# The max pass of an attention kernel in six groups of block pairs instead of eleven pairs, with a new order of all tasks

## The chip, the cores and the metric

The kernel runs on one core of one Trainium2 chip. The metric is the device time of one execution in microseconds, as the median of several runs. One execution was also recorded by the hardware profiler; all rows below are from that one.

## The reference, cut to what matters

```python
def _attn_ref(q, k, v, g_q, g_k):            # q, k, v: 8 x 12 x 448 x 64, fp32
    q_n, k_n = rmsnorm(q, g_q), rmsnorm(k, g_k)
    scores = 1/sqrt(64) * q_n @ k_n.T
    scores = scores - np.max(scores, axis=-1, keepdims=True)
    attn = np.exp(scores)
    attn = attn / (np.sum(attn, axis=-1, keepdims=True) + 1e-09)
    return attn @ v

def reference(...):
    x = attn_out.transpose(0, 2, 1, 3).reshape(3584, 768)
    # group router (4 groups), then expert router (4 experts a group), argmax each;
    # each token: combined * (relu(x @ w1[g, e]) @ w2[g, e]), w1 768x1024, w2 1024x768
```

## The kernel before, in words

The work has two stages that overlap a little: attention, and then a mixture of experts (MoE) on its output, sixteen experts of which each token takes one.

Attention is cut into 16 units, numbered u = 0 to 15; a unit is six heads of one batch. The rows of a unit's queries lie in 21 blocks of 128: for each of three pairs of heads seven blocks, of which the fourth (`TB`, block numbers 3, 10 and 17) is a tail block that holds 64 rows of either head. For a unit the kernel does this: it loads and normalizes k and q and transposes them (the tiles kt, kb, qa, qb); it makes a **max pass** (`plan_max`), in which TensorE multiplies each block of q by the 448 keys of its head (tile pmx, line 522, or line 517 for a tail block) and VectorE takes the maximum of each row (line 527, one reduction for a pair of blocks); the maxima are transposed (pmt) and join the operands of the **scores pass** (pss, lines 585 and 580), so that the exponential on ScalarE (line 595) already has its maximum subtracted; GpSimd or VectorE splits off the low part of the exponentials (pl, line 601); then TensorE multiplies by v (po, line 646), VectorE or ScalarE scales the result (lines 670, 671 or 666), and the output goes to HBM in two halves (xhl, lines 709 and 713). The router and the MoE stage (lines 1417 and 1444 are its two products) read it from there.

The products of the max pass of units 1 to 15 contract over 64 rows only. The two blocks of a pair use the lower and the upper 64 rows of the array (kt and kb hold the same keys in the two halves), so they run side by side. A tail block is two products of 64 columns, one for each head. All other products of the stage use all 128 rows.

PSUM has three buffers of two banks for all of this (`psd=3` in `ROOM`): pmx, pss, the transposes and the router's products take them in turn, so a task that takes one gets the buffer that the third taker before it used, and can start when that one's reader is through.

The order is written out by hand or by a planner outside the kernel: each step is a task with an engine, and `PLAN` gives each task a date (hundredths, in the order in which the tasks are added). `emit` sorts the tasks by their dates, so the dates set the order of the instructions on each engine and nothing else; a "*" picks the second engine for a task that may run on two (GpSimd or VectorE for the low parts, ScalarE or VectorE for the scaling). Each engine then works through its list strictly in that order, waiting on semaphores. The last MoE jobs, from the eleventh, are dated by a formula relative to the planned ones (`Moe.plan`).

In the list of before, a max task is one pair: 11 a unit, (0,1), (2,3), ... (18,19), (20), each of which takes one buffer.

Of the kernel before, what the change touches and what calls it, by code (L numbers as in the profile page):

```python
# [18 lines left out]
ALU = mybir.AluOpType  # L19
AX = mybir.AxisListType  # L20

P = 128
# [90 lines left out]
class Attention:  # L113
# [382 lines left out]

    def pairs_of(self, n, u):
        step = NBK if u == 0 else n
        return [(j, min(j + 2, o + step)) for o in range(0, n, step) for j in range(o, o + step, 2)]

    def plan_max(self, flow, u, B, D):
        nc = self.nc
# [3 lines left out]
        def mm(a, e):  # L506
            f = lambda t: t.rearrange("p n c -> p (n c)")
            s = d["mm", a] = self.ps_d.tile([P, 2, 512], F32, tag="psd", name=f"pmx{u}_{a}")
            for n in range(a, e):
                o = 64 * ((n - a) % 2)  # L510
# [3 lines left out]
                if c == TB:  # L514
                    for r in range(2):
                        x, z = self.blocks(i, r)
                        nc.tensor.matmul(s[r * 64:r * 64 + 64, n - a, 0:448],
                                         qa[:, n * P + r * 64:n * P + r * 64 + 64], kt[:, x:z],
                                         start=True, stop=True)
                else:  # L520
                    x, z = self.blocks(i, int(c > TB))
                    nc.tensor.matmul(s[:, n - a, 0:448], qa[:, n * P:(n + 1) * P], kt[:, x:z], start=True, stop=True)  # L522

        def rd(a, e):
            if "mx" not in d:
                d["mx"] = self.wl.tile([P, N], F32, tag="mx", name=f"mx{u}", bufs=self.ROOM["mx"])
            nc.vector.tensor_reduce(d["mx"][:, a:e], d.pop(("mm", a))[:, 0:e - a, 0:448], axis=AX.X, op=ALU.max)  # L527
# [16 lines left out]
        for a, e in self.pairs_of(N, u):  # L544
            b = Buffer("psd")
            x = flow.add("PE", lambda a=a, e=e: mm(a, e),
                         [*self.of(D, "kmv", a, e), *(self.of(D, "kcp", a, e) if u else []), *self.of(D, "qa", a, e), *firsts],
                         takes=[b] + ([] if a else [B["mx"]]), uses=[B["kt"], B["qa"]] + ([B["kb"]] if u else []))
            firsts = firsts or [x]
            reds.append(flow.add("DVE", lambda a=a, e=e: rd(a, e), [x, *reds[:1]],  # L550
                                 uses=[b, B["mx"]]))
        D["m"] = {}
        for a, e in ((0, 7), (7, 14), (14, 21)) if u == 0 else ((0, N),):
            bx, bm = Buffer("psd"), Buffer("mxt")
            need = [reds[j] for j, (x, z) in enumerate(self.pairs_of(N, u)) if x < e and z > a]
# [692 lines left out]
class Moe:  # L1248
# [222 lines left out]
    def plan_early(self, flow, attn, router, opens):  # L1471
# [13 lines left out]
        g = 0  # L1485
# [59 lines left out]
        self.g, self.last_tr = g, trs[-1]  # L1545
        self.at_read = {(j, i): mm[j, FC - 1] if i < 4 else m2s[j][-1] for j in range(self.JF) for i in range(len(PC))}

    def plan(self, agenda):
# [42 lines left out]
        for j, (k, later, c) in enumerate(J):  # L1591
# [66 lines left out]
441 1 3010 1825 439 4515 9008 12509 4716 963 3009 440 0 474 535 521 600 778 962 1026 1132 1607 1839* 1903 2503 1608  # L1658
1737 2349 1827 3012 475 568 1027 1079 1133 1185 1252 1436 1606 1671 1945 2010* 2454 2685 1736 2174 3366 2336 4127 898
1186 1422 1488 1469 1553 1738 1838 1902 2011 2013 2443* 2686 2874 2337 2395 2875 2502 6207 2012 2586 4938 4436 5381  # L1660
# [196 lines left out]
```

## Time and profile before

| what | value |
|---|---|
| median of 3 runs | 1008.05 us (1004.07 to 1014.55) |
| the profiled execution | 1012.01 us, its span 1010.4 us |
| PE (TensorE's products) busy in the span | 922.1 us, 91% |
| DVE (VectorE) busy | 745.2 us, 74% |
| ACT (ScalarE) busy | 623.8 us, 62% |
| POOL (GpSimd) busy | 566.0 us, 56% |
| last reduction of the max pass starts at | 450.9 us |

The busy times are shares of the whole span; the two stages have different limits, so the views by stretch are to be read beside them. PEld are weight loads; a product's row lasts from its first column in to its last column out, and rows overlap, so the distance from the start of one product to the start of the next tells what it costs the engine.

### The profile page before, as it was taken

To read this page: it belongs to the slowest core of one execution; us is meant where nothing else is said; L and a number is where in the kernel's file an instruction comes from. 1 tells how busy PE (TensorE), PEld (TensorE's weight loads), DVE (VectorE), ACT (ScalarE), POOL (GpSimd) and SP (SyncE) were. 2 spreads that over 40 slices of the span, in tenths; PEclk is the share of its full clock that TensorE was granted. 3 is DMA by queue.
4 is the path that set the end of the run, shared out by engine and by line. 5 is a ranking of instruction groups with operands and counts; after the bars stand their busy time and mean duration, and the time that the engine had idled before them with its cause. 6 is when DMAs were issued, how large, how long until landed. Compare 5 with 4: busy or idle time off the path is not lost.

```text
span 1010.4 us, 28824 instructions
## 1 busy us (share of the span) xinstructions
PE 922.1 (91%) x11761; PEld 656.8 (65%) x11761; DVE 745.2 (74%) x1002; ACT 623.8 (62%) x986; POOL 566.0 (56%) x481
## 2 busy tenths in 40 slices
PE   1699999999998989997896999999989999999995
PEld 1356666666665656655766776777757687778883
DVE  3999999899999899898775275566556785756620
ACT  3788998879987867657553264555446556445520
POOL 4589999989997878885445342223113232435411
PEclk9899999999998999899899999999989999999998
DMA  5776787787897467646897999997979999998910
GB/s 141 185 196 133 194 197 182 164 201 167 218 174 175 114 141 154 106 97 189 208 230 200 275 295 273 325 302 234 289 244 342 302 304 307 301 255 275 285 64 28
DMA packets 223095, 213.78 MB, mean 212 GB/s; under 512 B 129455, under 2 KB 179621, under 8 KB 222960
## 3 DMA queue, kind: packets, MB, share of 16 engines
q1 hardware_dynamic: 213008, 188.23, 70.7%
q0 software_dynamic: 8608, 22.99, 7.1%
q8 instruction: 93, 1.52, 0.7%
q10 hardware_dynamic: 1344, 0.69, 0.3%
q14 instruction: 42, 0.34, 0.1%
HBM read 145.69 MB, written 23.41 MB: 167 GB/s over the span
## 4 chain that ended last, share of the span: by engine, by line
PE 60%; DVE 19%; issue 7%; DMA 5%; ACT 4%; POOL 3%; SPq 2%; POOLq 0%; DVEq 0%; ACTq 0%
PE ps L1444 21%; PE ps L1417 20%; PE po L646 6%; DVE mx L527 5%; PE pss L585 5%; PE pmx L522 3%; DVE vl L374 3%; DVE ss L267 2%; DVE pl L601 2%; DMA nq<-q 1%; DMA stage<-w 1%; DMA tb<-tab 1%; PE pss L580 1%; ACT p L595 1%; PE pkt L303 1%
## 5 line engine op out<-in xcount | busy, mean ns | idle before, releaser
L601 POOL TENSOR_TENSOR pl<-p 128x896 f16<-128x896 f32 (+1 forms) x157 | 262.2, 1691 | 41.2 <-ACT p L595 38.1
L1417 PE MATMUL ps<-mx,w1h 128*128 128x256 f16 (+6 forms) x1728 | 245.1, 258 | 10.3 <-DMA mx<-xg 6.2
L1417 PE MATMUL ps<-mx,w1l 128*128 128x256 f16 (+6 forms) x864 | 212.2, 257 | 0.0
L527 DVE TENSOR_REDUCE mx<-pmx 128x2 f32<-128x896 f32 (+1 forms) x177 | 177.7, 1032 | 10.3 <-PE pmx L522 6.5
L595 ACT ACTIVATE p<-pss 128x896 f32<-128x896 f32 (+1 forms) x177 | 151.6, 884 | 52.8 <-PE pss L585 40.6
L646 PEld LDWEIGHTS <-p 128*128 128x128 bf16 (+1 forms) x3072 | 143.9, 103 | 51.2 <-issue 38.7
L1417 PEld LDWEIGHTS <-w1h 128*128 128x128 f16 x1728 | 155.9, 99 | 29.1 <-issue 14.1
L1444 PE MATMUL ps<-w2h,hh 128*128 128x384 f16 (+2 forms) x768 | 165.0, 306 | 6.9 <-ACT y L1456 6.9
L646 PE MATMUL po<-vh,pl 128*128 128x65 f16 (+1 forms) x1536 | 158.5, 196 | 11.5 <-DVE pl L601 6.1
L1444 PE MATMUL ps<-w2l,hh 128*128 128x384 f16 (+2 forms) x768 | 164.4, 304 | 0.0
L1444 PE MATMUL ps<-w2h,hl 128*128 128x384 f16 (+2 forms) x768 | 164.4, 304 | 0.0
L646 PE MATMUL po<-vh,p 128*128 128x65 f16 (+1 forms) x1536 | 160.9, 200 | 0.8 <-ACT xm L666 0.4
L646 PE MATMUL po<-vl,p 128*128 128x64 f16 (+1 forms) x1536 | 158.8, 196 | 0.0
L1371 DVE SCALAR_TENSOR_TENSOR w1l<-stage,w1h 128x1536 f16<-128x1536 f32 x64 | 113.5, 1797 | 47.9 <-ACT w1h L1369 46.6
L1371 DVE SCALAR_TENSOR_TENSOR w2l<-stage,w2h 128x1536 f16<-128x1536 f32 x64 | 111.5, 1754 | 50.5 <-ACT w2h L1369 50.4
L1444 PEld LDWEIGHTS <-hh 128*128 128x128 f16 (+2 forms) x1536 | 102.0, 101 | 65.1 <-issue 14.1
L1463 POOL DMA_INDIRECT out<-y,tb x23 | 36.7, 1594 | 185.5 <-ACT y L1456 117.0
L646 PEld LDWEIGHTS <-pl 128*128 128x128 f16 (+1 forms) x1536 | 129.2, 103 | 13.1 <-DVE pl L601 7.1
L1424 ACT ACTIVATE hh<-ps 128x256 f16<-128x256 f32 (+6 forms) x144 | 47.6, 348 | 128.4 <-PE ps L1417 119.1
L1369 ACT ACTIVATE w1h<-stage 128x1536 f16<-128x1536 f32 x64 | 93.6, 1480 | 34.9 <-DMA stage<-w 34.9
L585 PE MATMUL pss<-qa,kt 128*128 128x448 f16 x288 | 103.2, 358 | 3.3 <-DVE mx L527 2.1
L1406 POOL DMA_INDIRECT xg<-x,tb x41 | 60.8, 1482 | 80.7 <-DMA mx<-xg 33.8
(209 smaller groups left out, 1628.2 us busy)
## 6 DMA issues: line engine op xcount, KB each, us to landing
stage<-w SPq DMA_DIRECT2D x64, 768.0 KB, 10.2
stage<-w SPq DMA_DIRECT2D x64, 512.0 KB, 6.2
stage<-w SPq DMA_DIRECT2D x64, 256.0 KB, 5.1
vn<-v SPq DMA_DIRECT2D x16, 576.0 KB, 5.1
x<-xhl SPq DMA_DIRECT2D x16, 576.0 KB, 4.5
nk<-k SPq DMA_DIRECT2D x30, 288.0 KB
nq<-q SPq DMA_DIRECT2D x30, 288.0 KB, 3.8
qa<-qh SPq DMA_DIRECT2D x30, 176.0 KB, 3.2
```

The costliest lines, as they stand in the source:

```text
L527: nc.vector.tensor_reduce(d["mx"][:, a:e], d.pop(("mm", a))[:, 0:e - a, 0:448], axis=AX.X, op=ALU.max)
L585: nc.tensor.matmul(s[:, n - a, 0:448], w[:, n * P:(n + 1) * P], mv[:, x:z], start=first, stop=not first)
L595: nc.scalar.activation(p[:, 0:e - a], s, AF.Exp, scale=1.0 / 64)
L601: ENG[eng].tensor_tensor(l[:, 0:n], p[:, 0:n], h[:, 0:n], op=ALU.subtract)
L646: nc.tensor.matmul(o[op, c, 0:nn], w, mv, start=st, stop=sp, skip_group_check=True)
L1369: self.nc.scalar.activation(hi, t, AF.Copy, scale=64.0)
L1371: self.nc.vector.scalar_tensor_tensor(lo, t, 64.0, hi, op0=ALU.mult, op1=ALU.subtract)
L1406: self.nc.gpsimd.indirect_dma_start(g[0:m], None, self.x16[0:n], bass.IndirectOffsetOnAxis(ap=tb[0:m, i, 0:1], axis=0), bounds_check=n - 1 ...
L1417: nc.tensor.matmul(s[:, 0:c], wb[w][:, i, fs], x[:, l + i, o:o + c], start=i + j == 0, stop=i == DC - 1 and j == 2)
L1424: self.nc.scalar.activation(hh, s[:, 0:c], AF.Relu)
L1444: nc.tensor.matmul(s[q * m:q * m + m, 0:n], self.h[h][:, f, a:a + m], wb[w][:, f, o:o + n], start=f + j == 0, stop=f == self.FC - 1 and j ...
L1463: i = self.nc.gpsimd.indirect_dma_start(out, bass.IndirectOffsetOnAxis(ap=idx, axis=0), d.pop(("y", i))[:, 0:self.D // r], None, bounds_ch ...
```

## The change

For units 1 to 15 the max pass is made in six tasks instead of eleven. A task is a group of up to two pairs whose products stand one behind the other on TensorE, and it takes two PSUM buffers at once. Two of the tail blocks, 3 and 10, form a pair of their own, the third, 17, stands alone, and the other blocks are paired without them. There are still eleven reductions a unit, ten for pairs and one for a single block; that of (3,10) writes two columns that aren't neighbours. Each reduction is a task of its own, as before. Unit 0 keeps its pairs.

```diff
+    BATCHES = ((0, 1), (2, 4)), ((5, 6), (7, 8)), ((9, 11), (12, 13)), ((14, 15), (16, 18)), ((19, 20), (3, 10)), ((17,),)
...
-            for n in range(a, e):
-                o = 64 * ((n - a) % 2)
+            for m, n in enumerate(e):
+                o = 64 * m
...
+        def batch(b):
+            for ns in self.BATCHES[b]:
+                mm(ns[0], ns)
+
+        def rd(a, ns):
...
+            step = max(1, ns[-1] - a)
+            nc.vector.tensor_reduce(d["mx"][:, a:ns[-1] + 1:step], d.pop(("mm", a))[:, 0:len(ns), 0:448], axis=AX.X, op=ALU.max)
...
+            for j, ps in enumerate(self.BATCHES):
+                bs = [Buffer("psd") for _ in ps]
+                x = flow.add("PE", lambda j=j: batch(j),
+                             [y for nm in ("kmv", "kcp", "qa") for y in self.of(D, nm, 0, N)] + firsts,
+                             takes=bs + ([] if j else [B["mx"]]), uses=[B["kt"], B["qa"], B["kb"]])
+                firsts = firsts or [x]
+                for b, ns in zip(bs, ps):
+                    reds.append(flow.add("DVE", lambda ns=ns, o=0, w=len(ns): rd(ns[0], ns), [x, *reds[:1]],
+                                         uses=[b, B["mx"]]))
...
-        self.g, self.last_tr = g, trs[-1]
+        self.g, self.last_trs = g, trs
...
-                tg = max(tg, dated(self.last_tr) + 10.0)
+                tg = max(tg, max(map(dated, self.last_trs)) + 10.0)
```

`PLAN` is replaced as a whole: every task of both stages has a new date. The list has 75 tasks fewer, all of them max tasks on TensorE (15 units, 5 each). Read against the tasks, the two lists say the following. In the old one 165 max tasks of units 1 to 15 stand in 152 places on TensorE's list, that is with other products between them; in the new one 90 tasks stand in 88 places. Some steps change engine:

| step | old list | new list |
|---|---|---|
| low part of the exponentials (line 601), 177 tasks | 20 on VectorE | 16 on VectorE, the rest on GpSimd |
| low half of the output (line 713), 16 tasks of two instructions | 5 on VectorE | 2 on VectorE |
| scaling of the result, 48 tasks (one of lines 670 and 671 each on VectorE, seven of line 666 on ScalarE) | 19 on VectorE | 24 on VectorE |
| low part of k (line 298), units 1 to 15, 30 tasks | 3 on VectorE | 4 on VectorE |
| copy of the transposed k (lines 309, 311), 30 tasks | 1 on VectorE | 0 on VectorE |

## Rows read from the trace of the kernel before

**Rows 1.** Busy time by stretch: us from the start, busy (x instructions), clock, DMA.
```profile
75.00:450.00 375.00, 357.88 (x5814) 232.99 (x5812) 356.84 (x488) 304.79 (x538) 330.50 (x224) 0.98 0.73 162
450.00:553.00 103.00, 82.60 (x1097) 64.25 (x1096) 75.77 (x131) 53.76 (x99) 55.33 (x67) 0.94 0.78 196
553.00:1010.00 457.00, 438.85 (x4512) 335.04 (x4510) 255.22 (x302) 215.60 (x278) 135.97 (x117) 0.98 0.85 262
```

**Rows 2.** The chain that ended last, by line, from 75 to 450 us.
```profile
by line: PE po L646 14.6%; DVE mx L527 12.2%; PE pss L585 11.4%; DVE vl L374 7.5%; PE pmx L522 6.5%; issue 5.6%; DVE ss L267 3.9%; DVE pl L601 3.0%; PE pss L580 2.9%; DVE ql L336 2.7%; ACT p L595 2.5%; DVE qp L283 2.3%; PE pqt L324 2.3%; PE
```

**Rows 3.** The same chain from 450 to 553 us.
```profile
by line: issue 37.0%; DMA tb<-tab 12.2%; POOL pl L601 9.0%; POOL tab L1049 6.9%; DVE pl L601 6.3%; DMA mx<-xg 4.4%; DMA xg<-x,tb 2.9%; PE pss L585 2.7%; PE po L646 2.6%; POOL xg L1406 2.5%; DVE ogt L1154 2.3%; DVE vl L374 1.7%; DVE xg L1287
```

**Rows 4.** The same chain from 553 us to the end.
```profile
by line: PE ps L1444 46.9%; PE ps L1417 43.2%; DMA stage<-w 2.9%; issue 1.3%; DVE w1l L1371 1.2%; ACT w2h L1369 0.5%; DVE hl L1426 0.4%; DVE w2l L1371 0.4%; ACT y L1456 0.2%; SPq L1352 0.2%; POOL out L1463 0.2%; ACT hh L1424 0.1%; SPq L1353
```

**Rows 5.** Timeline of PE (start us, us) around a pair that stands alone.
```profile
228.70 0.19 PE L646 MATMUL po<-vl,p 128*128 128x64 f16 x1
228.73 0.20 PE L646 MATMUL po<-vh,pl 128*128 128x65 f16 x1
228.86 0.36 PE L522 MATMUL pmx<-kt,qa 64*128 64x448 f16 x1
228.86 0.36 PE L522 MATMUL pmx<-kb,qa 64*128 64x448 f16 x1
229.15 0.20 PE L646 MATMUL po<-vh,p 128*128 128x65 f16 x1
```

**Rows 6.** Timeline of PE from a pair of which one block is a tail.
```profile
313.96 0.36 PE L522 MATMUL pmx<-kt,qa 64*128 64x448 f16 x1
314.25 0.38 PE L517 MATMUL pmx<-kb,qa 64*64 64x448 f16 x2
314.56 0.36 PE L585 MATMUL pss<-qa,kt 128*128 128x448 f16 x1
314.76 0.35 PE L585 MATMUL pss<-qb,kb 128*128 128x448 f16 x1
```

**Rows 7.** Timeline of PE around two pairs, one behind the other.
```profile
196.81 0.19 PE L646 MATMUL po<-vh,pl 128*128 128x65 f16 x1
196.94 0.36 PE L522 MATMUL pmx<-kt,qa 64*128 64x448 f16 x1
...
197.13 0.35 PE L522 MATMUL pmx<-kt,qa 64*128 64x448 f16 x1
...
197.42 0.20 PE L646 MATMUL po<-vh,p 128*128 128x65 f16 x1
```

**Rows 8.** The tile pmx: its reductions, ns min/median/max, first and last start.
```profile
L527 DVE TENSOR_REDUCE mx<-pmx x177: 608/1082/1094, 32.9 to 450.9; 128x2 f32<-128x896 f32 x159, 128x1 f32<-128x448 f32 x18
```

**Rows 9.** Groups by line: busy us, mean ns of one, idle before.
```profile
L601 POOL TENSOR_TENSOR pl<-p 128x896 f16<-128x896 f32 (+1 forms) x157 | 262.2, 1691 | 41.2 <-ACT p L595 38.1 <-ACT rl L987 2.2 <-PE po L646 0.4
...
L666 ACT ACTIVATE xm<-po,rr 128x64 f32<-128x64 f32 x203 | 44.8, 335 | 13.1 <-DVE rt L1038 5.5 <-DVE po L280 4.2 <-DVE rr L652 3.2
...
L601 DVE TENSOR_TENSOR pl<-p 128x896 f16<-128x896 f32 (+1 forms) x20 | 33.0, 1657 | 2.5 <-ACT p L595 2.5
L713 POOL TENSOR_TENSOR xhl<-xm,xhl 128x1152 f16<-128x1152 f32 (+1 forms) x22 | 33.0, 1520 | 1.5 <-ACT xhl L709 1.4
...
L713 DVE TENSOR_TENSOR xhl<-xm,xhl 128x1152 f16<-128x1152 f32 (+1 forms) x10 | 12.3, 1269 | 2.8 <-ACT xhl L709 2.8
L670 DVE TENSOR_TENSOR xm<-po,rr 128x384 f32<-128x384 f32 x19 | 10.4, 550 | 0.2
...
L671 DVE TENSOR_TENSOR xm<-po,rr 128x64 f32<-128x64 f32 x19 | 4.0, 213 | 0.0
L298 DVE TENSOR_TENSOR kn<-nk,kn 128x448 f16<-128x448 f32 x3 | 3.1, 1021 | 0.0
```

**Rows 10.** What PE waited for from 75 to 450 us: us in total, times, longest.
```profile
PE pmx L522 <- DVE mx L527: 5.9, 5, 4.1
...
PE pmx L522 <- DVE ql L336: 1.9, 3, 1.4
PE pss L585 <- DVE mx L527: 1.9, 4, 1.0
```

More of the change, by code (lines that the diff above doesn't have):

```diff
@@ L521, in mm @@
                     x, z = self.blocks(i, int(c > TB))
-                    nc.tensor.matmul(s[:, n - a, 0:448], qa[:, n * P:(n + 1) * P], kt[:, x:z], start=True, stop=True)
-        def rd(a, e):
+                    nc.tensor.matmul(s[:, m, 0:448], qa[:, n * P:(n + 1) * P], kt[:, x:z], start=True, stop=True)
+        def batch(b):
+            for ns in self.BATCHES[b]:
+                mm(ns[0], ns)
+        def rd(a, ns):
             if "mx" not in d:
                 d["mx"] = self.wl.tile([P, N], F32, tag="mx", name=f"mx{u}", bufs=self.ROOM["mx"])
-            nc.vector.tensor_reduce(d["mx"][:, a:e], d.pop(("mm", a))[:, 0:e - a, 0:448], axis=AX.X, op=ALU.max)
+            step = max(1, ns[-1] - a)
+            nc.vector.tensor_reduce(d["mx"][:, a:ns[-1] + 1:step], d.pop(("mm", a))[:, 0:len(ns), 0:448], axis=AX.X, op=ALU.max)
         def fin0(a, e):
@@ L543, in plan_max @@
         reds, firsts = [], []
[L544 to L551, printed above, removed]
+        if u == 0:
+            for a, e in self.pairs_of(N, u):
+                b = Buffer("psd")
+                x = flow.add("PE", lambda a=a, e=e: mm(a, range(a, e)),
+                             [*self.of(D, "kmv", a, e), *self.of(D, "qa", a, e), *firsts],
+                             takes=[b] + ([] if a else [B["mx"]]), uses=[B["kt"], B["qa"]])
+                firsts = firsts or [x]
+                reds.append(flow.add("DVE", lambda a=a, e=e: rd(a, range(a, e)), [x, *reds[:1]],
+                                     uses=[b, B["mx"]]))
+        else:
+            for j, ps in enumerate(self.BATCHES):
[3 more added lines that the diff above has]
+                             takes=bs + ([] if j else [B["mx"]]), uses=[B["kt"], B["qa"], B["kb"]])
+                firsts = firsts or [x]
+                for b, ns in zip(bs, ps):
+                    reds.append(flow.add("DVE", lambda ns=ns, o=0, w=len(ns): rd(ns[0], ns), [x, *reds[:1]],
+                                         uses=[b, B["mx"]]))
         D["m"] = {}
@@ L554, in plan_max @@
             bx, bm = Buffer("psd"), Buffer("mxt")
-            need = [reds[j] for j, (x, z) in enumerate(self.pairs_of(N, u)) if x < e and z > a]
+            need = [reds[j] for j, (x, z) in enumerate(self.pairs_of(N, u)) if x < e and z > a] if u == 0 else reds
             x = flow.add("PE", lambda a=a, e=e: fin0(a, e), need, takes=[bx], uses=[B["mx"]])
@@ new lines @@
+58241 62096 62623 62230 62426 60683 63382 65729 65860 63850 65759 65861 64370 65788 66011 65732 65859 66010 65863
+66164 66382 66008 66216 66703 66158 66307 66351 66383 66457 66701 67066 67070* 67254 67849 68455 67848 68414 70850
+64500 64913 66161 63334 64910 64984 63983 65888 66163 63982 64234 65731 66160 66486 66704 65862 66165 67145 66159
+66700 67850 68413 68803 69200 61986 63852 65733 65735 66009 66487 68138 68194 67071 68302 68411 67644 68098 68152
+68153 68629 68802 68301 68630 68974 68628 68749 68975 68748 68972 69197 68973 69196 69256 69350 69760* 69894 70304*
@@ L1803 @@
+70849 70305 72017 70848 72204* 73244 66850 67065 68303 67645 68412 68452 66162 66849 67852 67851 68454 68627 71341
+71589 71765 69198 69761 69835 69255 70695 71763 69199 69236 69399 65730 66217 68976 66702 68453 65736 69237 71291
+71340 69762 71258 71305 70694 71343 71414 71342 71588 71762 71413 71968 72016 71587 71764 71844 71761 71936 72110
+71935 72109 72157 72203 72613 72614 73023* 73114 73245 73648 73731
 """
```

108 lines of the change are left out of this document (52 added, 56 removed), and 171 rows, old and new, of the table PLAN.

## The prediction

> **What bounds the kernel now.** I read the busy times by stretch first, because the max pass exists only in the first half: its last reduction starts at 450.9 us [rows 8]. From 75 to 450 us no engine has much room: PE 357.9, VectorE 356.8 and GpSimd 330.5 of 375 us [rows 1]. PE's busy share overstates, since rows overlap; so I go on to the chain of work that ended last, in the same stretch. It changes sides all the time: of the lines shown, PE has 14.6 + 11.4 + 6.5 + 2.9 + 2.3 = 37.7%, VectorE 12.2 + 7.5 + 3.9 + 3.0 + 2.7 + 2.3 = 31.6%, and GpSimd none [rows 2]. The reader is to see that a microsecond taken from one engine here is not a microsecond of the kernel: by the chain it is about 0.38 for PE and 0.32 for VectorE. The stretch from 450 to 553 us is a chain of latencies, issue 37.0% and DMA and GpSimd steps of the router [rows 3]. After that PE sets the end alone, 46.9 + 43.2 = 90.1% of the chain in the two products of the MoE [rows 4]; none of that work changes, so it starts earlier or later with what stands before it. The third reading is the timeline of PE around single pairs, which prices the change.
>
> **PE: visits to the 64-row shape.** In front of a pair that stands alone the last full product starts at 228.73 and the pair at 228.86, 0.13 us, where the product before it took 0.03; behind it the next product starts 0.29 later [rows 5]. Two pairs one behind the other show what a pair itself takes: 0.19 from the first to the second, and again 0.29 from the second to the full product [rows 7]. So a visit costs 0.10 going in and 0.10 coming out, and each pair in it 0.19. A pair with a tail block takes 0.29 to its quadrant products and 0.31 from these to the next full one [rows 6], 0.60 instead of 0.29: 0.31 for the turn between the two shapes.
>
> Before, by the list: 152 visits x 0.20 = 30.4, 165 pairs x 0.19 = 31.4, and three pairs a unit with a turn inside, 45 x 0.31 = 14.0; together 75.8 us. After: 88 x 0.20 = 17.6, the same 165 x 0.19 = 31.4, and one turn a unit, from (19,20) to (3,10), 15 x 0.31 = 4.7; together 53.7. **PE is spared 22.1 us** over units 1 to 15. The pair (3,10), four quadrant products, isn't in the trace: if its two halves ran one after the other it would cost up to 0.29 more [rows 6], 15 x 0.29 = 4.4 us; I take 0, because both the two column halves [rows 6] and the two row halves [rows 5] start within 0.01 us. On the chain at 0.377, 22.1 us are worth 8.3.
>
> **PE: two buffers at once.** Here is the price. A buffer comes back after its last product and one reduction, 0.36 [rows 5] + 1.08 [rows 8], about 1.4 us; the exponential is of the same size. I walked both lists in their order and added up, for each taker of a buffer, PE's work between the end of the third taker before it and its own start: 0.76 for a pair of scores (four products 0.19 apart), 0.37 for a group of twelve po products 0.03 apart, the visits as above, and for transposes and router 0.2 to 0.8, estimated from the number of their products at such spacings. In the old list 70 of 464 takers come after less than 1.4 us, short by 21.0 us in all; in the new one 155 of 463, short by 57.5 us. The reason is plain: a group asks for two of the three buffers at one time, so the second is the one that the second-last taker used, and until VectorE has made both reductions the scores and transposes have one buffer to turn over. How much of a shortage becomes a wait the old trace tells: waits of PE that end with a reader of its buffers are 5.9 + 1.9 + 1.9 = 9.7 us [rows 10], about half of the 21.0, since a wait once taken gives the next taker slack. The added 36.5 at the same half are **18 us of waits more**. Bounds: 0, if the new dates put enough of other engines' work in order around the groups, and 36.5. Queued behind a waiting group on PE are po groups that need no buffer; who waits for them is the scaling and with it the two po banks. Net on PE: -22.1 + 18 = -4.1, on the chain at 0.377 **-1.6 us**.
>
> Beside it one sentence of the notes: the Trainium skill, TensorEngine Tiling (Array Packing), section PSUM Bottleneck, says that tiling speeds up TensorE but not the emptying of PSUM, which may then become the bottleneck; by it the 8.3 us would be 0, and the rows of VectorE above lean its way.
>
> **VectorE: the steps that change engine.** The reductions stay 11 a unit at the same size; the strided output of (3,10) is two columns, which I cost at nothing (one element a row more or less in a 1.08 us instruction). Moved: four low parts away, -4 x 1.66 = -6.6; three output halves of two instructions, -3 x 2 x 1.27 = -7.6; five scalings to it, +5 x (0.55 + 0.21) = +3.8; one low part of k, +1.0 [all rows 9]. VectorE is spared 9.4 us, at 0.316 of the chain **-3.0 us**. GpSimd gets 4 x 1.69 + 6 x 1.52 = 15.9 us more [rows 9]; what hides it is its idle time, 375 - 330.5 = 44.5 us [rows 1], 41.2 of which over the run lie before its low parts, waiting for ScalarE [rows 9]. If that cover is gone, it costs up to 15.9. ScalarE loses 5 x 7 x 0.335 = 11.7 us [rows 9], worth nothing on this chain.
>
> **The rest of the new dates.** Loads, stores, router steps and the first ten MoE jobs are reordered too, SP's and GpSimd's DMA issues among them; the trace of before can't show what a new order does. The place where it would tell is the stretch of latencies, 103 us with 37.0% of issue [rows 1, 3]. I take 0 and allow 10 either way, about a quarter of its 38 us of issue time. The later date of the MoE's gathers changes the order of a few transfers that run long before PE needs them: 0.
>
> **The sum.** The profiled execution took 1012.01 us, 1.6 more than its span, which I leave as it is: 1012.01 - 1.6 (PE) - 3.0 (VectorE) = 1007.4. The profiled one lies 4.0 us above the median of the runs, so I forecast 1003 us. A measurement of this kernel can't tell less than about 1% from no change: the three runs span 10 us.
>
> **The rivals.**
> *The buffers suffice.* If the new order hides the turn-over of buffers, nothing is given back: -8.3 - 3.0 = -11.3, that is 997; and if PE is in truth the pacer of the whole stretch, all 22.1 + 3.0 come, 983. For it: PE waits visibly for buffers only 9.7 us in 375 now, and a group puts two reductions in front of VectorE at once. Against it: VectorE is as full as PE.
> *VectorE paces.* Nothing that PE saves counts, since VectorE is busy 95% of the stretch with reductions that don't change: 1008 - 3 = 1005 at best, 1008 if GpSimd takes its share back. This is the rule of the page named above, worked out here.
> *The ring of three becomes the bound.* The slow one: every shortage is paid, 36.5 us, and since PE then waits for VectorE's second reduction and VectorE for PE's next group, they are on the chain in full: 36.5 - 22.1 = +14.4, 1022. It decides from the point where more than 22 of the 36.5 us come back as waits, six tenths, against the five that the old trace shows. For it: 66 of the 150 buffers that the groups take come too early by the count above, against 24 of 177 for the old pairs.
> That the change doesn't do what it says can be left aside: the number of visits is fixed by the list.
>
> **How the numbers follow.** Forecast (partly given back, 998 to 1010) 0.35; buffers suffice (983 to 1000) 0.33; VectorE paces (1003 to 1010) 0.12; ring of three (1012 to 1030) 0.20. Faster by over 1% means under 998: the rival's 0.33 less a little, and a few of the forecast's with a better order in the latencies, 0.36. Slower by over 1% is over 1018: most of the last case, some of it from the reordered stretch, 0.19. Within 1% is the rest, 0.45. The range leaves out a tenth on either side: 984, close to the end of the fast rival, to 1020.
>
> **What would show it.** In the profile after, the max products should stand in some 88 visits, with two pairs 0.19 apart and 0.60 or less from (19,20) to the end of (3,10); the last reduction should start 5 us earlier than 450.9, and the MoE's dense part by as much. Waits of PE for mx, ql and p would tell the price: near 28 us for the forecast, under 12 for the fast rival, over 45 for the slow one. The forecast is wrong above all if the half that I took from the old trace for shortage and wait doesn't hold for groups, or if the stretch of latencies moves by more than its 10 us.

## The result and the profile after

The changed kernel takes 1018.71 us (median of 16 runs, 1012.38 to 1026.13), the kernel before, run beside it, 1008.16 (16 runs, one of them, at 3666.76, far from the others); the ratio is 1.0115, 95% interval 1.0087 to 1.0144. The forecast was 1003, the range 984 to 1020: the time lies inside the range and on the wrong side of no change. The profiled execution has a span of 1021.7 us.

Max-pass lines are now 524 and 519 (products) and 534 (reductions), the scores 603 and 598, the low part 619, the products with v 664, the MoE products 1435 and 1462. Busy time of the changed kernel by stretch, as [rows 1]:

```profile
75.00:450.00 375.00, 339.21 (x5717) 224.30 (x5714) 353.69 (x486) 299.01 (x513) 336.14 (x228) 0.97 0.72 161
450.00:553.00 103.00, 84.50 (x1177) 64.88 (x1173) 77.66 (x131) 53.54 (x95) 65.65 (x68) 0.96 0.84 214
553.00:1010.00 457.00, 443.42 (x4468) 336.19 (x4472) 256.06 (x304) 216.19 (x277) 129.54 (x119) 0.97 0.88 259
```

PE is 18.7 us less busy from 75 to 450 us, VectorE 3.2 less, GpSimd 5.6 more. But the window is fixed and the changed kernel is behind in it (5717 products, 5814 before), so what the visits are worth is read from the max products alone (tile pmx), first before, then after (length, PE busy, VectorE busy, clock, DMA share, GB/s):

```profile
0.00:500.00 500.00, 81.83 (x384) 177.66 (x177) 0.96 0.73 167
0.00:500.00 500.00, 62.42 (x384) 174.95 (x177) 0.97 0.72 165
```

They take 19.4 us less of PE. Yet the last reduction stands at 459.0, 8.1 us later than in [rows 8], where 5 us earlier was forecast (the old attention list has it between 446.6 and 452.1 in six other traces below, the new one at 459.0 and 455.9 in two):

```profile
L534 DVE TENSOR_REDUCE mx<-pmx x177: 574/1081/1094, 30.3 to 459.0; 128x2 f32<-128x896 f32 x159, 128x1 f32<-128x448 f32 x18
```

The timeline of PE around a last group, (19,20) and (3,10), shows that the visits cost what was worked out: 0.29 from the last full product to the pair, 0.29 to the quadrant products and 0.32 back to a full one (0.61 from the pair on, 0.60 forecast), and the four quadrant products start within 0.01 us. The list of PE's products holds 88 visits, before 152.

```profile
201.83 0.35 PE L603 MATMUL pss<-qb,kb 128*128 128x448 f16 x1
202.12 0.36 PE L524 MATMUL pmx<-kt,qa 64*128 64x448 f16 x1
...
202.41 0.38 PE L519 MATMUL pmx<-kt,qa 64*64 64x448 f16 x2
202.42 0.38 PE L519 MATMUL pmx<-kb,qa 64*64 64x448 f16 x2
202.73 0.21 PE L664 MATMUL po<-vh,p 128*128 128x65 f16 x1
```

The chain that ended last from 75 to 450 us, as [rows 2]:

```profile
by line: POOL pl L619 16.0%; DVE mx L534 10.8%; PE po L664 6.9%; issue 6.3%; PE pss L603 5.2%; DVE vl L374 4.2%; POOL xhl L731 3.6%; ACT p L613 3.5%; POOL tab L1067 2.6%; DMA qb<-ql 2.5%; POOL kn L298 2.3%; DMA qa<-qh 2.2%; DVE ss L267 1.9%
```

Of the lines shown PE has 6.9 + 5.2 = 12.1% where it had 37.7; GpSimd, none among those shown before, has 16.0 + 3.6 + 2.6 + 2.3 = 24.5%. What PE waited for in that stretch (total, times, longest), as [rows 10]:

```profile
PE po L664 <- POOL pl L619: 7.0, 12, 1.3
PE pmx L519 <- DVE mx L534: 6.3, 1, 6.3
PE pss L603 <- DVE mx L534: 4.6, 7, 2.6
PE pkt L303 <- DVE mx L534: 4.1, 1, 4.1
PE pmx L524 <- DVE mx L534: 2.8, 2, 2.3
```

The low parts on GpSimd, 0.2 us before, are now the largest wait. Up to the last product with v, which starts at 492.65 us before and at 493.39 after, PE is busy 12.8 us less and idle 74.4 us instead of 60.8, 13.6 more: what the visits gave, the waits took.

```profile
0.00:492.65 492.65, 431.82 (x6760) 280.10 (x6761) 452.30 (x620) 379.39 (x657) 403.09 (x334) 0.97 0.73 165
0.00:493.39 493.39, 419.00 (x6761) 274.15 (x6761) 452.89 (x616) 370.93 (x616) 414.71 (x340) 0.97 0.71 164
```

Attention ends nearly where it did: the first MoE product starts at 493.9 us (492.8 before). From there to the end the changed kernel needs 527.8 us, the kernel before 517.5. That is where these two profiles have the loss. Both lengths vary from trace to trace, though: with the old attention list the first MoE product starts between 486.5 and 493.9 us in six other traces, and with the old experts' list the rest takes 513.0 (e1) to 520.3 us (e4) in e1 to e8, and up to 528.1 (e12) in runs beside which the kernel before was slower too. What doesn't vary is the stretch from the first product of the sixth MoE job to that of the tenth: 114.7 us in all eleven traces with the old experts' list, 125.3 here. What PE waited for from 480 to 1010 us, first after, then before:

```profile
PE ps L1435 <- DMA mx<-xg: 13.9, 4, 4.5
PE ps L1435 <- DVE hl L1444: 6.8, 6, 3.7
```
```profile
PE ps L1444 <- ACT y L1456: 6.9, 3, 5.0
PE ps L1417 <- DMA mx<-xg: 6.2, 1, 6.2
```

And the chain of the last stretch, as [rows 4]; gathers (xg) and transposes (mx), not in that row before, have 12.8%, and the two products 62.8 instead of 90.1:

```profile
by line: PE ps L1462 33.1%; PE ps L1435 29.7%; DMA xg<-x,tb 7.8%; issue 6.9%; DMA stage<-w 6.8%; DMA mx<-xg 5.0%; DMA out<-y,tb 1.7%; DVE w2l L1389 1.6%; DVE w1l L1389 1.3%; ACT w2h L1387 0.9%; POOL out L1481 0.8%; SPq L1535 0.8%; ACT w1h L
```

Pieces of that chain before the seventh job's first product (start, us), and GpSimd in that time:

```profile
616.83 13.91 DMA xg<-x,tb
630.75 5.03 DMA mx<-xg
636.62 5.95 DMA xg<-x,tb
642.60 3.38 DMA mx<-xg
646.11 4.96 PE ps L1435 x18
```
```profile
636.62 2.16 POOL L1424 DMA_INDIRECT xg<-x,tb  x1 [11.03 <-DVE hl L1444]
```

The job's last gather goes out at 636.62, its transpose lands at 645.98, and PE has nothing to do from 641.8 on.

### The profile page after: what moved, and what is told of

The parts are those of the page before. It is cut to its first block, busy times and chain, and to the rows that moved or that the text cites. A ratio compares the mean times of both kernels' runs of the same rounds, so it can differ in the third digit from the quotient of the medians.

```text
span 1021.7 us, 28764 instructions
## 1 busy us (share of the span) xinstructions
PE 913.6 (89%) x11761; PEld 651.9 (64%) x11761; DVE 746.2 (73%) x1002; ACT 617.9 (60%) x952; POOL 577.2 (56%) x490
## 4 chain that ended last, share of the span: by engine, by line
PE 38%; DMA 19%; DVE 15%; POOL 11%; issue 7%; ACT 6%; SPq 3%; POOLq 0%; DVEq 0%; ACTq 0%
PE ps L1462 15%; PE ps L1435 14%; POOL pl L619 6%; DVE mx L534 5%; DMA xg<-x,tb 5%; DMA mx<-xg 4%; DMA stage<-w 3%; PE po L664 3%; PE pss L603 3%; DVE vl L374 2%; ACT p L613 2%; POOL xhl L731 1%; DMA nq<-q 1%; DVE ss L267 1%; DMA nk<-k 1%
## 5 line engine op out<-in xcount | busy, mean ns | idle before, releaser
L619 POOL TENSOR_TENSOR pl<-p 128x896 f16<-128x896 f32 (+1 forms) x161 | 269.9, 1698 | 40.4 <-ACT p L613 39.8
L1435 PE MATMUL ps<-mx,w1h 128*128 128x256 f16 (+6 forms) x1728 | 248.9, 260 | 21.0 <-DMA mx<-xg 13.9
L1435 PE MATMUL ps<-mx,w1l 128*128 128x256 f16 (+6 forms) x864 | 214.4, 260 | 0.3 <-DVE w1l L1389 0.3
L534 DVE TENSOR_REDUCE mx<-pmx 128x2 f32<-128x896 f32 (+1 forms) x177 | 174.9, 1033 | 8.5 <-PE pmx L524 4.7
```

What stands on the lines that cost most here:

```text
L534: nc.vector.tensor_reduce(d["mx"][:, a:ns[-1] + 1:step], d.pop(("mm", a))[:, 0:len(ns), 0:448], axis=AX.X, op=ALU.max)
L619: ENG[eng].tensor_tensor(l[:, 0:n], p[:, 0:n], h[:, 0:n], op=ALU.subtract)
L1435: nc.tensor.matmul(s[:, 0:c], wb[w][:, i, fs], x[:, l + i, o:o + c], start=i + j == 0, stop=i == DC - 1 and j == 2)
```

## The experiments

Two theories of the loss stood at the start. **Two buffers**: a group takes two of the three PSUM buffers, VectorE gives them back one reduction after the other, and PE waits. **The new dates**, of the attention half or of the experts' half (the MoE), cost by themselves. Where a list of dates was mixed with other tasks, tasks whose operands or buffers weren't ready at their date moved back to the first place that is free. Each ratio is to the kernel before as it ran beside the experiment: its median was 1008.27 us beside e1 to e4, 1007.18 beside e5 to e8, 1015.23 beside e9 to e12, 1006.79 beside e13 to e16 and 1013.34 beside e17 and e18. Ratios can be compared across these groups, microseconds of their traces only with that in mind.

### Each half of the list alone

e1 has the changed attention with the experts' half in the order of before; e2 and e5 the attention of before with the experts' half in the new order. In e2 the old rule for the late jobs' gathers was left in, and one of them overwrites its buffer before it is read, so that it multiplies other rows; e5 has the new rule and replaces it.

```diff
 PLAN, e1: attention: new dates
-          experts' half: new dates
+          experts' half: old dates, shifted with the first product
 PLAN, e2: attention: old dates
-          experts' half: old dates
+          experts' half: new dates, shifted with the first product
 e5 besides:
-        self.g, self.last_tr = g, trs[-1]
+        self.g, self.last_trs = g, trs
```

> The attention stage with the six groups and its new order; the MoE tasks in the order of the kernel before, their dates shifted by the 18.23 us by which the new list dates the first MoE task later. Theory A, the MoE order: in the traces the first MoE product starts at 492.8 before and 493.9 after, so the 11 us are lost behind it, where PE waits for gathers; then this kernel ends within 3 us of before (ratio 0.997 to 1.003). Theory B, the attention order: the max pass ends 8 us later and the router, the stores and so all transfers of the MoE with it; then this kernel is as slow as the changed one, ratio 1.008 or more.

> The complement: the attention stage of the kernel before, eleven pairs in their old order; the MoE tasks in the order of the changed kernel, shifted by -18.23 us. Theory A, the MoE order: about 1.010, PE waiting for gathers between 600 and 780 us as in the changed kernel. Theory B, the attention order: within 0.3% of before.

> As the complement before it (attention in the order of the kernel before, MoE in that of the changed kernel), but with the changed rule for the gathers, which the new MoE dates need: without it a late gather stands ahead of the transpose that empties its buffer, and e2_old_att_new_moe gathers other rows. If the new MoE order costs by itself what the traces say, 527.7 against 517.5 us from the first MoE product to the end, the ratio is 1.006 to 1.010, since the first product also starts some 4 us sooner. If it costs nothing beside the old attention: within 0.3% of before.

Measured: e1 1.0055 [1.0029, 1.0081], e2 1.0162 [1.0114, 1.0209], e5 1.0145 [1.0106, 1.0183]. From the first MoE product to the end e1 takes 513.0 us, e2 528.4, e5 526.0. So the new list of the experts' half suffices alone for the whole loss: 1.45% beside the old attention, and 0.60% (1.0115 - 1.0055) beside the changed one. The changed attention loses some 5 us instead of gaining, between what the two theories of e1 had. The two halves don't add up (0.55 + 1.45 = 2.0% against 1.15), so neither is a price that holds beside any other half.

The new list of the experts' half is more than an order: it gives 16 of the 64 evictions of the experts' second product (y) to the other engine, eight each way between ScalarE and VectorE. The table of steps that change engine leaves them out, and no run separates them from the dates.

### Groups and tails without the new dates

e3 pairs the tails with each other and leaves eleven tasks, each at its old place: the turns inside pairs go (14.0 us of the 22.1), no task takes two buffers. e4 makes the six groups, each where its last pair stood; e11 where its first pair stood (with 109 other tasks that had to move).

```diff
 e3:
+    BATCHES = ((0, 1),), ((2, 4),), ((5, 6),), ((7, 8),), ((9, 11),), ((3, 10),), ((12, 13),), ((14, 15),), ((16, 18),), ((19, 20),), ((17,),)
 e4, e11:
+    BATCHES = ((0, 1), (2, 4)), ((5, 6), (7, 8)), ((9, 11), (12, 13)), ((14, 15), (16, 18)), ((19, 20), (3, 10)), ((17,),)
```

> The order of the kernel before, date for date, with the new pairing alone: eleven pairs of which (3,10) is a pair of tails and (17) stands alone, each its own task in the place of an old pair. It takes the 45 turns of shape inside a pair away, 45 x 0.31 = 14.0 us of PE, and no buffer is taken sooner or later. If PE's time is worth 0.377 by the chain: 5 us faster, ratio 0.995. If VectorE and GpSimd set the pace: no change. If PE sets it: 14 us, 0.986.

> The order of the kernel before in all but the max pass, with the six groups: of a unit's eleven places in the old order, two that follow each other become one group at the place of the second; 14 tasks had to move, by 12 us of dates together. PE is spared about 22 us as in the change, and two buffers are taken at once. If half of the added shortage becomes waiting, as forecast: 1 to 2 us faster. If the buffers suffice: 8 us faster, 0.992. If the ring of three buffers binds: up to 14 us slower, 1.014.

> Six groups in the order of before, as in the run of the groups in the old order (1.0118), but each group where its first pair stood instead of its last, with the few steps that it needs moved ahead of it. Theory 'delay' (a group's first pair waits for the last one's place, so bounds and scores come late): 0.995 to 1.003, close to the tails paired alone. Theory 'ring' (a group holds two of three buffers while two reductions of 1.09 us pass): 1.008 to 1.02, TensorE waits in 75 to 450 us near 45 us as before, since the place in the order does not give a buffer back sooner.

Measured: e3 0.9987 [0.9957, 1.0017], e4 1.0118 [1.0075, 1.0161], e11 1.0236 [1.0202, 1.0270]. In e3 the max products take 13.1 us less of PE than before (81.8):

```profile
0.00:500.00 500.00, 68.67 (x384) 177.06 (x177) 0.95 0.73 168
```

and the kernel gains 1.3 us, at most 4.3 by the interval. At the forecast's 0.377 it would have been 14.0 x 0.377 = 5.3, or 4.9 with the 13.1, a little outside. The groups then cost 13 us over the tails alone (1.0118 - 0.9987 = 0.0131 of 1008). An earlier place didn't help but cost more than either theory had allowed; a list with 109 displaced tasks tells little about groups.

### Shorter reductions

e6 and e7 are e3 and e4 with reductions over 224 of the 448 keys in units 1 to 15; e18 and e17 do the same to the kernel before and to the changed kernel, each with its own dates. The maxima are then those of half the keys.

```diff
-...[:, 0:len(ns), 0:448], axis=AX.X, op=ALU.max)
+...[:, 0:len(ns), 0:448 if u == 0 else 224], axis=AX.X, op=ALU.max)
```

> e3_tails_only with reductions of half length in units 1 to 15: the maximum is taken over 224 of the 448 keys, so the kernel leaves out half of the maximum (the shift of the softmax). A reduction takes about 0.6 instead of 1.08 us, so each buffer of the max pass comes back 0.5 us sooner and VectorE is spared some 80 us. It is the base for the next run. VectorE as pacer: 15 us faster or more than e3_tails_only; if other engines pace: under 8.

> e4_groups_old_order with the same half reductions (half of the maximum left out). Theory ring: what costs e4 its 13 us over e3 is that two of three buffers are out until VectorE has made two reductions; with reductions of 0.6 us two are done in the time of one, and the difference to e6 falls to 5 us or less. Rival, delay: the cost comes from the first pair of each group standing later in the order, so the maxima come later whatever a reduction takes; then 10 us or more stay.

> The same edit in the kernel before, the yardstick of the run above (reductions over 224 keys of 448, part of the computation is left out). Both theories: ratio 0.986 to 0.992, as for the tails paired alone with short reductions (0.989).

> The changed kernel with its own dates, untouched but for the reductions of the max pass, which read 224 keys of 448 (part of the computation is left out; the reductions take some 0.62 us instead of 1.08). Ring theory (a group waits because two buffers are given back one reduction after the other): the changed kernel gains clearly more by it than the kernel before does by the same edit, 18 to 24 us against 9 to 14, last product with the values near 474 us, ratio to the kernel before 0.987 to 0.995. Misfit theory (the loss is that of an order not fitted to its work, whatever the reductions take): it gains what the kernel before gains, ratio 0.997 to 1.004.

Measured: e6 0.9890 [0.9849, 0.9931], e7 0.9940 [0.9916, 0.9964], e18 0.9917 [0.9886, 0.9949], e17 1.0084 [1.0050, 1.0117]. In the old order the price of the groups falls from 13 us to 5 (0.9940 - 0.9890), as two buffers had it, though by the intervals this fall of 8 us is only just told from none. In the kernels' own orders it isn't so: the kernel before gains 0.83%, the changed one, which by two buffers should have gained twice as much, 0.31% (1.0115 to 1.0084), not told from nothing and by the two intervals at most 0.75%. Both theories had it gain at least what the kernel before gains; both miss. Its chain, and below it that of e18, from 75 to 450 us:

```profile
by line: POOL pl L619 18.7%; PE po L664 11.1%; issue 8.1%; PE pss L603 7.6%; DVE vl L374 4.7%; POOL xhl L731 3.9%; POOL kn L298 3.8%; ACT p L613 3.7%; PE pmx L524 2.8%; ACT xm L684 1.9%; DVE mx L534 1.9%; PE pss L598 1.9%; DMA qb<-ql 1.8%; 
```
```profile
by line: PE po L646 24.1%; PE pss L585 16.4%; PE pmx L522 10.3%; DVE vl L374 6.6%; PE pss L580 4.1%; issue 3.6%; PE pmx L517 3.2%; PE pkt L303 2.9%; PE pqt L324 2.6%; DVE pl L601 2.4%; POOL pl L601 2.4%; DVE ss L267 2.4%; ACT p L595 2.2%; D
```

With the reductions out of the way PE sets the pace of the kernel before (63.6% in the lines shown). In the changed kernel the reductions fall from 10.8 to 1.9% of the chain and GpSimd takes their place; PE's idle time in the stretch goes from 375 - 339.2 = 35.8 us to 375 - 337.7 = 37.3, and its wait for the low parts grows from 7.0 to 10.3:

```profile
75.00:450.00 375.00, 337.72 (x5728) 224.15 (x5727) 301.83 (x488) 297.32 (x509) 336.88 (x230) 0.97 0.73 164
PE po L664 <- POOL pl L619: 10.3, 14, 2.6
```

So in the changed kernel it isn't the length of the reductions that makes PE wait. What the longest waits stand behind can be read from its trace: the low part of v (vl, line 374), an instruction of VectorE that comes ahead of the reductions. There are 32 of one size, and the longest takes nine times the shortest; first before, then after:

```profile
L374 DVE SCALAR_TENSOR_TENSOR vl<-vn,vh x32: 906/1082/6262, 55.3 to 466.2; 128x768 f16<-128x768 f32 x32
L374 DVE SCALAR_TENSOR_TENSOR vl<-vn,vh x32: 907/1292/8035, 49.0 to 467.3; 128x768 f16<-128x768 f32 x32
```

The longest one of the changed kernel, with GpSimd in that time and PE's wait behind it:

```profile
326.48 9.86 POOL L619 TENSOR_TENSOR pl<-p 128x896 f16<-128x896 f32 x6
336.31 1.87 POOL L298 TENSOR_TENSOR kn<-nk,kn 128x896 f16<-128x896 f32 x1
...
330.96 8.04 DVE L374 SCALAR_TENSOR_TENSOR vl<-vn,vh 128x768 f16<-128x768 f32 x1
338.92 3.08 DVE L534 TENSOR_REDUCE mx<-pmx 128x2 f32<-128x896 f32 x3
...
340.05 0.58 PE L519 MATMUL pmx<-kt,qa 64*64 64x448 f16 x2 [6.32 <-DVE mx L534]
```

GpSimd works without a break, seven steps in these rows, and vl ends at 339.00, 0.82 us after the last of them (338.18). Two more vl of the changed kernel last 6.20 us (from 103.53) and 5.62 us (from 398.17), again beside a row of GpSimd's steps, and PE's waits of 4.07 and 2.57 us follow them. So 13.0 of the 17.8 us of waits for the maxima listed above stand behind three long vl. The kernel before has one, 6.26 us, with a wait of 4.11 us behind it. In e17 they last 6.36, 9.23 and 5.61 us, and the waits behind them are 12.6 us: shorter reductions don't shorten these. All 32 together take 49.2 us of VectorE before and 60.6 after. That vl is held up by GpSimd's unbroken work is read from this coincidence; no run changes it alone.

### The steps that change engine

e8 is e1 with four low parts and three output halves back from GpSimd to VectorE and five scalings back to ScalarE. e12 is e3 with such a move forward: four low parts (units 4, 8, 9, 12) and three output halves (units 5, 10, 13) from VectorE to GpSimd. The scalings stay, so VectorE is spared 6.6 + 7.6 = 14.2 us and not the 9.4 of the expectation.

```diff
 PLAN, e8, four low parts and three output halves:
-<date>
+<date>*
 PLAN, e12, four low parts and three output halves:
-<date>*
+<date>
```

> e1_new_att_old_moe with the old shares of the engines: four low parts of the exponentials and three output halves go back from GpSimd to VectorE, five scalings from VectorE to ScalarE, at the same places of the order. In the trace of e1 GpSimd's low parts are 16.2% of the chain from 75 to 450 us, before they were not among its lines. If GpSimd has become the pacer of the new order: 3 to 5 us faster than e1. If VectorE is: 3 us slower. If the buffers are: the same within 2 us.

> Tails paired with each other, two buffers never taken at once, order of before (0.9987 without more), and the four low parts and three output halves that the new dates take from VectorE given to GpSimd (about 9.4 us off VectorE, 16 us onto GpSimd). Theory 'VectorE is the next bound after TensorE': 3 to 5 us faster than the tails alone, ratio 0.994 to 0.997. Theory 'GpSimd has no room at these places' (low parts of 2.9 us and more that TensorE then waits for): 1.000 to 1.006.

Measured: e8 1.0109 [1.0073, 1.0145], 5 us more than e1 (0.54%, by the intervals only just told from none); e12 1.0073 [1.0045, 1.0102], 9 us more than e3. What PE waited for from 75 to 450 us, first e3, then e12:

```profile
PE po L664 <- POOL pl L619: 1.0, 3, 0.5
```
```profile
PE po L664 <- POOL pl L619: 9.1, 11, 2.3
```

Much the same move is worth a gain of 5 us in the new order and a loss of 9 in the old one. In the new one the theory that GpSimd paces it, taken from its 16.2% of the chain, fails by its sign. In the old one the loss is visible: PE waits 8.1 us more for GpSimd's low parts, which I had costed at nothing.

### The gathers of the experts' half

e9 has the attention of before and the experts' half at the new dates, except the job rows, gathers and transposes, which keep the old order; e10 has only these at the new dates. e13 is the changed kernel with the rows, gathers and transposes of the seventh to tenth job at their old distance; e14 the kernel before with those of the same four jobs at the new one.

```diff
 PLAN, e13, jobs 7 to 10, rows, gathers, transposes:
-new dates
+old dates, shifted with the first product
 PLAN, e14, the same tasks:
-old dates
+new dates, shifted with the first product
```

> Attention exactly as before; in the second half the weight loads, splits, evictions and scatters at the new dates, but the loads of the job rows, the gathers of tokens and their transposes in the order of before. Theory A (late gathers on GpSimd hold TensorE up at the jobs between 611 and 816 us): the loss of 1.0145 that the new dates of the second half cost alone goes, ratio 0.997 to 1.005, first product of the experts to the end about 517 us, TensorE waits for gathered tokens near 6 us instead of 13.9. Theory B (the order of the weight loads and splits is what costs): ratio stays 1.010 to 1.016, first product to end about 526 us.

> The complement: everything in the order of before, with the loads of the job rows, the gathers and their transposes alone at the new dates. Theory A (late gathers): ratio 1.008 to 1.016, first product to end 525 us or more. Theory B (weight loads and splits): 0.997 to 1.004, first product to end about 517 us. Between the two: the two together make the loss, neither alone.

> The changed kernel, with only the job rows, gathers and transposes of the four jobs whose first products stand late in its trace (the seventh to the tenth job, first products at 646 to 737 us) back at the distance that they had in the order of before. Theory A (these gathers hold TensorE up): the stretch from the sixth to the tenth job's first product falls from 125 us to about 115 us as before, and the ratio from 1.0115 to 1.000 to 1.005. Theory B (the new order of weights and splits, or a list that no longer fits together): the stretch may shorten, but as much is lost elsewhere between the first product and the end, which stays near 527 us, ratio 1.009 to 1.014.

> The complement: the kernel before, with only the rows, gathers and transposes of these four jobs at the new dates. Theory A: the stretch from the sixth to the tenth job's first product grows from 115 to 122 us or more, ratio 1.006 to 1.012. Theory B: stretch within 3 us of before, ratio 0.998 to 1.004.

Measured: e9 1.0129 [1.0103, 1.0156], e10 1.0081 [1.0050, 1.0111], e13 1.0240 [1.0201, 1.0280], e14 1.0011 [0.9987, 1.0035]. The distances between first products of the sixth, tenth and twelfth job in the traces, in us:

| | first to 6th | 6th to 10th | 10th to 12th | 12th to the end |
|---|---|---|---|---|
| before | 117.4 | 114.7 | 81.4 | 204.1 |
| after | 117.6 | 125.3 | 79.6 | 205.4 |
| e5 | 117.4 | 126.5 | 77.4 | 204.8 |
| e9 | 122.9 | 115.6 | 91.2 | 206.3 |
| e10 | 128.8 | 123.1 | 75.0 | 205.3 |
| e13 | 117.3 | 116.4 | 91.7 | 204.6 |
| e14 | 115.7 | 130.1 | 75.4 | 204.0 |

By their ratios e9 fits theory B and e10 theory A: each part of the new list costs by itself beside the rest of the old one. The late gathers do hold PE up from the sixth to the tenth job: with them it takes 123 to 130 us, without them 115 to 116, whatever the rest. The first column says less, since the old experts' list itself takes 113.2 to 126.9 us there in the other traces. But e9 and e13, which take the late gathers away, lose as much before the twelfth job. Where it goes in e13, by PE's wait and VectorE's timeline:

```profile
746.90 0.48 PE L1462 MATMUL ps<-w2h,hh 128*128 128x384 f16 x1 [11.76 <-DVE y L1476]
```
```profile
741.22 1.76 DVE L1389 SCALAR_TENSOR_TENSOR w1l<-stage,w1h 128x1536 f16<-128x1536 f32 x1 [14.09 <-ACT w1h L1387]
742.90 1.75 DVE L1389 SCALAR_TENSOR_TENSOR w2l<-stage,w2h 128x1536 f16<-128x1536 f32 x1
744.57 1.75 DVE L1389 SCALAR_TENSOR_TENSOR w1l<-stage,w1h 128x1536 f16<-128x1536 f32 x1
746.24 0.61 DVE L1476 TENSOR_SCALAR y<-ps,tb 128x384 f32<-128x384 f32 x1
```

PE waits 11.76 us for a buffer of the second product, whose eviction (y) stands on VectorE behind three splits of weights, and the first of these behind a load of weights of the new order, which in the chain runs from 731.67 for 6.64 us. That y is also one of the 16 that changed engine: in the kernel before ScalarE makes it, at 740.97; whether it would have come sooner there isn't tested. Before that wait e13 is 14.0 us ahead of the changed kernel (the group of products in which it falls starts at 731.08, there at 745.06), 3.4 of them from an earlier first MoE product, behind it 0.8 (the next group at 752.16 and 753.00). So gathers and weights are late together, and moving one uncovers the other. Two limits of this reading: e13's profiled execution was the fastest of its six (1022.24, median 1029.22), so the runs lose 7 us more than the trace shows; and e14's was the slowest of its twelve (1014.43, median 1009.32), so that late gathers alone, 130.1 us in its trace, cost the runs nothing that can be measured (at most 0.35%).

### Two controls

e15 and e16 are the kernel before with the dates of one half moved at random by up to 1.5 us each way; the work is the same. In e15 314 tasks then had to move by more than 0.5 us, in e16 26; in the end 61 tasks of e15 stand more than 1.5 us from their old date, up to 6.3, and none of e16.

```diff
 PLAN, e15, attention; e16, experts' half:
-<date>
+<date> + uniform(-1.5, 1.5)
```

> A control: the kernel before, with nothing changed but every date of the attention half moved at random by up to 1.5 us, the same work with neighbours swapped. It tells how much of the runs with the old order is the price of an order that is not fitted to its own work. If the order is not that sensitive: 0.997 to 1.004, last reduction within 3 us of 450.9. If it is: 1.005 to 1.015, and the 12 us of the groups in the old order could not be put down to the buffers alone.

> The same control for the second half: the kernel before, with every date of the experts' half moved at random by up to 1.5 us and the attention half untouched. Not sensitive: 0.997 to 1.004, first product to end near 517 us. Sensitive: 1.005 or more, 522 us or more, and then the 10 us that the new dates of this half cost need no single cause.

Measured: e15 1.1562 [1.1514, 1.1610], last reduction at 601.4; e16 1.0169 [1.0136, 1.0203], first product to end 535.8 us. Both far outside "not sensitive". Random moves of 1.5 us among the experts cost more than the whole change does; in the attention half the moves, some of them larger, cost fourteen times as much. So a mixed list (e4, e7, e9 to e11, e13) carries a price of its own, and e4's 13 us can't be put down to buffers; the runs that keep a list whole (e1, e3, e5, e6, e8, e12, e17, e18) weigh more.

No run beats both kernels with the whole computation: e3, at 0.9987, is the kernel before within its error.

## Why the prediction was wrong

**Visits.** Right: 88 in the list, 0.10 going in, 0.61 for the turn and the way out against 0.60, no extra cost for (3,10). The max products take 19.4 us less of PE, where 22.1 were forecast.

**What PE's time is worth.** Too high. The forecast took PE's 37.7% of the chain as the price of every microsecond taken from it. e3 spares 14.0 us in the old places (13.1 in its rows) and gets 1.3, interval up to 4.3. A share of a chain says who ended the waits, not what happens when that engine gets faster: another engine's piece may be ready to end them. That VectorE's pieces did so here is argued, not shown.

**Two buffers.** The size was near, 18 us of waits forecast, 13.6 us more of idle time in the trace; the mechanism was another, so that is luck. PE's waits for the maxima that are listed grew from 5.9 + 1.9 in [rows 10] to 6.3 + 4.6 + 4.1 + 2.8 = 17.8, and for the low parts from 0.2 to 7.0. The forecast let a buffer come back one reduction of 1.08 us after its products. But 13.0 of the 17.8 us stand behind three vl of 5.6 to 8.0 us in front of the reductions, which it didn't count, and halving the reductions (e17) left PE's idle time at 37.3 us (35.8) and brought 0.3%, where the kernel before gains 0.8. The rival "the ring of three becomes the bound" names 1022, close to the time, for a reason that e17 doesn't bear out. In the old order (e4 to e7) the reductions did count for 8 of 13 us, in a list that carries the price of mixing.

**VectorE paces.** This rival forecast 1005 at best and no loss over 1008; PE's saving did count for nothing, but the time went beyond it. Its premise misreads a row: VectorE is busy 95% of the stretch, but reductions are 154.8 of these 356.8 us. The Trainium skill, TensorEngine Tiling (Array Packing), section PSUM Bottleneck, says that tiling doesn't speed up the emptying of PSUM, whose copy may become the bottleneck after a fourfold speedup of TensorE. By that rule, taken for the smaller speedup here, e17 should have gained more than e18. It didn't, 0.31% against 0.83, so no run here shows the rule to be this kernel's loss; that e3's saving on PE came to 1.3 us, and that shorter reductions speed up the kernel before, agrees with it.

**The engine moves.** VectorE's relief was forecast at -3.0, GpSimd's load at 0 because 44.5 us of idle time hide it. In the new order the move is worth 5 us (e8 against e1), so there the term held. In the old one it costs 9 (e12 against e3), and "what hides it is its idle time" fails: GpSimd idles 375 - 330.5 = 44.5 us before, and PE yet waits 8.1 us more for low parts. An idle sum says nothing of whether the single low part is ready when PE asks for it. Nor did VectorE get its 9.4 us: the 32 vl take 11.4 us more of it in the changed kernel (60.6 - 49.2).

**"The rest of the new dates": 0, and the later gathers: 0.** This is the step that failed and on which the sign turned. The profile puts +10.3 us between the first MoE product and the end (527.8 - 517.5), the stretch from the sixth job to the tenth alone +10.6 (125.3 - 114.7), and e5, with the attention of before, costs 1.45%. I had named the ten planned jobs as reordered but looked for the risk only in the stretch of latencies, where attention hands over, and held that the gathers "run long before PE needs them"; PE waits 13.9 us for them, 6.2 before. The gathers are only the visible half: with them back in their places PE waits in the tenth job for an eviction behind the weights' splits (e13). The attention list adds its share: e1 loses 0.55%, some 5 us, where -1.6 - 3.0 = -4.6 us was forecast.

**What stays open.** Whether a list exists in which the groups pay. The controls show that the order of the experts' half can lose 17 us by moves of 1.5 us, so that its loss needs no single cause beside those that e13 shows; how much of it the 16 evictions make that changed engine isn't known. The attention half's loss in e1 (0.55%) has waits for the low parts and for the maxima, most of the latter behind long vl; none of them was taken away by itself.

## What to carry to other kernels

When a change replaces a fitted order as a whole, price the order before the operations: every stage whose dates are new, also those whose work is untouched, is a term with a range as wide as what a small random move of that stage costs, here 17 us in one half and far more in the other. A share of the chain isn't an exchange rate, and an idle sum isn't a cover; look at how long before its reader each piece ends. An experiment that mixes two orders needs a control in which only the order is disturbed.

## What the runs showed of the hardware that was not expected

A short wait of TensorE costs more than itself. In the changed kernel it has nothing to do from 641.8 to 646.11 us (the row says 4.29), having been busy for nearly all of the 28 us before at a granted clock of 1.00; in the windows behind it (length, PE busy, ..., clock, DMA share, GB/s) the granted clock is 0.52 and 0.62, that is mostly the lower level of 1.2 GHz instead of 2.4:

```profile
640.00:644.00 4.00, 1.82 (x27) 1.62 (x24) 3.43 (x4) 3.02 (x6) 3.39 (x4) 1.00 0.45 158
644.00:648.00 4.00, 1.89 (x8) 1.09 (x9) 0.68 (x3) 0.11 (x1) 1.30 (x2) 0.52 0.86 192
648.00:652.00 4.00, 4.00 (x19) 2.28 (x18) 0.00 (x0) 0.00 (x0) 0.00 (x0) 0.62 1.04 398
```
```profile
646.11 0.69 PE L1435 MATMUL ps<-mx,w1h 128*128 128x320 f16 x2 [4.29 <-DMA mx<-xg]
...
650.86 0.40 PE L1462 MATMUL ps<-w2h,hh 128*128 128x384 f16 x1
...
654.84 0.44 PE L1435 MATMUL ps<-mx,w1h 128*128 128x320 f16 x2
...
657.28 0.33 PE L1462 MATMUL ps<-w2h,hh 128*128 128x384 f16 x1
```

The 18 products behind the wait take 650.86 - 646.11 = 4.75 us, 18 products of the same size in the next group, at a clock of 1.00 again, 657.28 - 654.84 = 2.44. So 2.3 us more are lost, and the wait of 4.29 us cost some 6.6.

An instruction of VectorE can take nine times its usual time beside a busy GpSimd. The rows of vl under "Shorter reductions" show 8.04 us instead of 0.91, ended 0.82 us after a row of seven GpSimd steps; 9.23 us in e17 likewise. A busy time of VectorE that counts such instructions says little of the work in it.

One execution is no measure of a stage either: with the same attention half, the last product with v starts at 492.65 us in the trace of the kernel before, and at 487.2 in e10, 486.3 in e16 and 493.8 in e5, where that half is untouched.
